# Soft-cap attention and a bilinear FFN on one core: first k load in two parts, cap loaded first, raw weights from the fifth on issued by SP

## The chip, the cores and the metric

The kernel runs on 1 core of one Trainium2 chip. The metric is device time in microseconds (us) of one execution, the median of several runs. A profile is one execution recorded by the hardware profiler. Its span goes from the first to the last instruction of the program.

## What is computed

```python
scale = 1.0 / np.sqrt(q.shape[-1])
scores = scale * np.matmul(q, k.transpose(0, 1, 3, 2))
scores = cap * np.tanh(scores / cap)
attn = softmax(scores)                       # exp, sum, divide
x = (attn @ v) -> 1792 tokens x 768
out = (x @ w_a) * (x @ w_b) @ w_out
```

q, k and v are 4 batches x 12 heads x 448 x 64 in float32, cap is one number, w_a and w_b are 768 x 1536 and w_out is 1536 x 768. The weights are float64: each raw weight block is loaded as pairs of 32-bit words and turned into float32 on the chip.

## The kernel before, in words

The 48 heads are worked in 24 pairs (`NPAIR`), two heads one above the other on the 128 partitions. The first 12 pairs (`NPG`) are group 0, the other 12 are group 1. For one pair `pi`:

- `load_k` (L204) loads k and q, each with four DMAs of 32 partitions, as blocks of 32 x 32 (packets of 128 bytes); `load_v` (L222) loads v. `turn` (L234) transposes the blocks on DVE, which gives k and q with the head's dimension on the partitions.
- `scores` (L258) multiplies them on PE in four chunks c, in the order 0, 1, 3, 2. `tanh` (L277) and `exp` (L285) run on ACT: tanh per chunk, exp per half (`hf`, two chunks). Two PSUM slots hold the scores, so chunk 3 waits for the tanh of chunk 0, and so on.
- `attend` (L301) multiplies with v on PE, in two halves. `add_full` and `add_last` (L289, L296) sum the probabilities on DVE, `sums` (L320) finishes the sum on PE.
- The sum's reciprocal goes through DRAM to reach all partitions: `recip` (L331, DVE), `store_rec` (L340, SP writes rd), `load_den` (L343, SP reads den back, two DMAs). Then `scale` (L356, DVE) gives x, and in group 0 `split_x` (L370, DVE) splits it into xhi and xlo, the operands of the FFN.

The FFN of a group needs the x of its pairs. `hidden` (L455) is one block of the first layer (18 matmuls in a row, tiles pha and phb), `project` (L486) one of the second layer. Its second token half (h = 1) needs xhi and xlo of pairs 6 to 11, pair 11 in the last three of its 18 matmuls. Weights come in the order `seq`, numbered t: `load64` (L385) loads the raw block (768 KB: 6 DMAs of 128 KB for t < 4, else 2 of 384 KB), `conv` (L402) makes float32 of it (two steps on ACT, three on DVE, one on POOL), `split_hi` and `split_lo` (L433, L443) make the PE operands. Two raw blocks fit at a time.

The order of work is planned before the program is written. Each step is a `job` with an engine, a cost, a lag and needs. The PE order is written out by hand (L663 to L701): it alternates `scores_of`, `attend_of`, `sums_of` and, from pair 12 on, pieces of the FFN (`ffn(us)` puts pieces worth that many us of PE). Every other engine takes, at each moment, the job with the earliest due time among those that can start. The loop at L824 writes all jobs in the order found, and each engine executes its own list in order. An engine's DMAs are issued in that list too. The semaphores of SP's and ACT's DMAs are eight in number and used in turn, so the ninth DMA of the two engines together is not issued before the first has landed.

`warm_up` (L741) issues memsets and matmuls on zeros before the first data. `limits` (L757) makes from cap the scale factors that tanh and exp read.

Of the kernel before, what the change touches and what calls it, by code (L numbers as in the profile page):

```python
# [119 lines left out]
def kernel(  # L120
# [403 lines left out]
    def loads(pi, heads):  # L524
        pairs = range(pi, pi + heads)
        for nm in "kq":
            eng = "ACT" if nm == "q" and pi < 2 else "SP"
            for n in range(P // BLK):
                free = [("turn", nm, p - NP) for p in pairs] if pi < NPG else [("turn", nm, pi - 1)]
                needs = [("load", nm, pi, n - 1)] if n else free  # L530
                job(("load", nm, pi, n), eng, 0.52, load_k, (pi, nm, n, heads), needs, 3.2 if pi < 2 else 4.0)
                jobs["load", nm, pi, n].order_only = n > 0
# [37 lines left out]
    def turns(pi):  # L570
        for nm in "kq":
            free = [("scores", pi - 2, c) for c in range(SUB)] + [("lo", nm, pi - 1)]
            job(("turn", nm, pi), "DVE", 0.56, turn, (pi, nm), [*(("load", nm, pi, n) for n in range(P // BLK)), *free])
# [85 lines left out]
    SOON, RAW, BACKLOG = 4.0, 24.0, 3.0  # L659
# [3 lines left out]
    for pi, heads in ((0, 1), (1, 1), *((i, 2) for i in range(2, NPG, 2)), *((i, 1) for i in range(NPG, NPAIR))):  # L663
# [22 lines left out]
    for pi in range(NPG, NPAIR + 1):  # L686
# [5 lines left out]
        if pi < NPAIR:  # L692
# [5 lines left out]
            ffn(GAP / 2 if pi > NPG else 7.2)  # L698
# [13 lines left out]
    for t, (nm, f, g) in enumerate(seq):  # L712
        if g == 0:
            parts = 6 if t < 4 else 2
            for n in range(parts):
                needs = [("raw", t, n - 1)] if n else [("conv", t - 2, 5)]
                job(("raw", t, n), "POOL" if t < 6 else "SP", 0.8 if t < 6 else 0.5, load64, (t, n, parts), needs, 4.0, RAW + 6.0 * (t + n / parts) if t < 4 else 0.0)
                jobs["raw", t, n].order_only = n > 0
            steps = (("ACT", 0.82), ("ACT", 0.8), ("DVE", 0.48), ("DVE", 0.48), ("DVE", 0.88), ("POOL", 2.1))
            for n, (eng, us) in enumerate(steps):  # L720
# [3 lines left out]
                job(("conv", t, n), eng, us, conv, (t, n), needs, 0.5)  # L724
# [15 lines left out]

    def warm_up():  # L741
        warm = bank(0, "warm")
        nc.vector.memset(psum[0][:, 0], 0.0)
        for n in (S, S, S, S // 2):
            nc.tensor.matmul(warm[:, :n], psum[0][:, 0, :P], psum[0][:, 0, :n], start=True, stop=True)
# [3 lines left out]
        nc.vector.memset(sel, 0.0)  # L749
        for z in kz:  # L750
            nc.vector.memset(f32(z), 0.0)
        nc.vector.memset(sel[:, Q - QS : Q], 1.0)
        nc.vector.memset(both, 0.0)
        for j, o in enumerate(own):
            nc.vector.memset(both[o, Q + (j - 1) * QS : Q + j * QS], 1.0)

    def limits():  # L757
# [5 lines left out]
        nc.vector.tensor_scalar_mul(capt[:, 1:2], capt[:, 6:7], 1.0 / math.sqrt(D))  # L763
        nc.scalar.activation(capt[:, 7:8], capt[:, 0:1], AF.Exp, scale=-1.0)
# [129 lines left out]
```

## Time and profile before

| | us |
|---|---|
| median of 3 runs | 717.94 |
| lowest, highest | 716.88, 720.42 |
| the profiled execution | 718.51 |
| its span | 716.7 |
| PE busy in the span | 703.4 (98%) |

A row of a timeline gives start, duration, engine, line, operation, output<-input, shape, count, and in brackets the idle time of the engine just before it with what ended it. The q behind an engine's name (SPq, ACTq) marks DMAs that it issues: the duration is that of issuing, not of the transfer. PEld is the loading of weights into PE, which overlaps the matmuls.

### The profile page before, as it was taken

The numbers are of one execution on the slowest core, as the hardware profiler recorded it, in microseconds if no ns is written. First come the engines' busy times: TensorE is split into PE (matmuls) and PEld (weight loads), VectorE is DVE, ScalarE is ACT, GpSimd is POOL, SyncE is SP. The second block draws the span as 40 slices with busy tenths as digits, with TensorE's granted clock in tenths as the row PEclk, the third lists the DMA queues.
The fourth block names the chain that finished last, engine by engine and source line by source line (L and its number), as shares of the span: only waits on it lengthen the run. The fifth ranks groups of instructions, "written<-read, shape, count | busy, mean of one in ns | idle before, by whom it ended". The sixth has DMA issues, their size and how long they took to land.

```text
span 716.7 us, 11238 instructions
## 1 busy us (share of the span) xinstructions
PE 703.4 (98%) x4370; PEld 578.3 (81%) x4370; DVE 423.0 (59%) x649; ACT 347.7 (49%) x474; POOL 112.0 (16%) x104
## 2 busy tenths in 40 slices
PE   7999998999999999999999999999999999999996
PEld 2333356879879789779879779999999999999996
DVE  4678897676679688686974849432043424434232
ACT  5989986577777566575646630222321112202100
POOL 0536431231322222222221100000000000000000
PEclk9999999999999999999999999999999999999999
DMA  9999585758777857858646437331022013101013
GB/s 128 152 171 170 140 212 123 193 143 200 184 170 193 193 141 177 201 138 227 157 116 159 146 101 248 110 109 45 11 83 83 23 34 99 53 15 44 1 45 113
DMA packets 142739, 90.55 MB, mean 126 GB/s; under 512 B 108024, under 2 KB 128536, under 8 KB 142680
## 3 DMA queue, kind: packets, MB, share of 16 engines
q1 hardware_dynamic: 135784, 82.53, 46.8%
q0 software_dynamic: 3040, 6.79, 4.0%
q10 hardware_dynamic: 3856, 0.46, 0.5%
q8 instruction: 36, 0.59, 0.4%
q14 instruction: 23, 0.19, 0.1%
HBM read 67.24 MB, written 22.50 MB: 125 GB/s over the span
## 4 chain that ended last, share of the span: by engine, by line
PE 92%; DMA 3%; SPq 2%; DVE 1%; ACT 1%; issue 0%; ACTq 0%; DVEq 0%
PE pv L308 10%; PE po L493 8%; PE po L494 8%; PE po L495 8%; PE phb L460 8%; PE phb L462 8%; PE phb L461 8%; PE pha L460 8%; PE pha L462 8%; PE pha L461 8%; PE psc L266 5%; PE psc L271 3%; DMA den<-rd 2%; PE pv L329 2%; SPq L220 1%; PE psc L274 1%
## 5 line engine op out<-in xcount | busy, mean ns | idle before, releaser
L493 PE MATMUL po<-who,gh 128*128 128x384 f32 x336 | 113.4, 337 | 0.0
L495 PE MATMUL po<-who,gl 128*128 128x384 f32 x336 | 112.5, 335 | 0.0
L494 PE MATMUL po<-wlo,gh 128*128 128x384 f32 x336 | 112.5, 335 | 0.0
L460 PE MATMUL pha<-xhi,wha 128*128 128x448 f32 x288 | 105.0, 365 | 2.7 <-DVE xhi L374 2.7
L460 PE MATMUL phb<-xhi,whb 128*128 128x448 f32 x288 | 105.2, 365 | 0.0
L462 PE MATMUL pha<-xhi,wla 128*128 128x448 f32 x288 | 104.8, 364 | 0.0
L461 PE MATMUL pha<-xlo,wha 128*128 128x448 f32 x288 | 104.6, 363 | 0.2 <-DVE xlo L375 0.2
L462 PE MATMUL phb<-xhi,wlb 128*128 128x448 f32 x288 | 104.6, 363 | 0.0
L461 PE MATMUL phb<-xlo,whb 128*128 128x448 f32 x288 | 104.3, 362 | 0.0
L283 ACT ACTIVATE pf<-psc,capt 128x896 f32<-128x896 f32 (+1 forms) x96 | 84.3, 909 | 29.6 <-PE psc L271 19.3
L308 PE MATMUL pv<-pf,vb 128*64 128x448 f32 x384 | 78.8, 553 | 0.0
L287 ACT ACTIVATE pf<-pf,capt 128x1792 f32<-128x1792 f32 (+1 forms) x48 | 77.1, 1606 | 0.8
L504 DVE TENSOR_TENSOR acc<-po,acc 128x384 f32<-128x384 f32 x84 | 46.4, 553 | 43.0 <-PE po L495 42.9
L467 ACT COPY asb<-pha 128x448 f32<-128x448 f32 x48 | 25.4, 531 | 81.8 <-PE pha L462 81.0
L493 PEld LDWEIGHTS po<-who,gh 128*128 128x128 f32 x336 | 63.1, 188 | 2.4 <-issue 1.2
L494 PEld LDWEIGHTS po<-wlo,gh 128*128 128x128 f32 x336 | 63.1, 188 | 0.1
L495 PEld LDWEIGHTS po<-who,gl 128*128 128x128 f32 x336 | 63.1, 188 | 0.0
L308 PEld LDWEIGHTS pv<-pf,vb 128*64 128x64 f32 x384 | 25.8, 139 | 45.5 <-issue 38.0
L477 DVE TENSOR_TENSOR asb<-phb,asb 128x448 f32<-128x448 f32 x48 | 29.9, 622 | 53.4 <-PE phb L462 53.4
L460 PEld LDWEIGHTS pha<-xhi,wha 128*128 128x128 f32 x288 | 54.0, 187 | 8.8 <-DVE xhi L374 3.4
L460 PEld LDWEIGHTS phb<-xhi,whb 128*128 128x128 f32 x288 | 54.0, 187 | 6.4 <-issue 2.5
L479 ACT CAST gh<-asb 128x448 fp32r<-128x448 f32 x48 | 27.2, 566 | 66.0 <-DVE asb L477 65.6
(103 smaller groups left out, 1038.4 us busy)
## 6 DMA issues: line engine op xcount, KB each, us to landing
w64o<-in_moe_w_out_dram SPq DMA_DIRECT2D x24, 384.0 KB
w64a<-in_moe_w_a_dram SPq DMA_DIRECT2D x18, 384.0 KB
w64b<-in_moe_w_b_dram SPq DMA_DIRECT2D x18, 384.0 KB
den<-rd SPq DMA_DIRECT2D x48, 112.0 KB
out_dram<-acc SPq DMA_DIRECT2D x13, 384.0 KB
wda<-wta SPq DMA_DIRECT2D x12, 384.0 KB
wdb<-wtb SPq DMA_DIRECT2D x12, 384.0 KB
wdo<-wto SPq DMA_DIRECT2D x12, 384.0 KB
```

Source lines behind the costliest of these rows:

```text
L266: nc.tensor.matmul(to, tk[o, at : at + (P if full else R)], tq[o], start=True, stop=True)
L283: nc.scalar.activation(to, prob.pop((pi, "s", c))[:, :n, :S], AF.Tanh, scale=capt[:, 1:2])
L287: nc.scalar.activation(pf, pf, AF.Exp, scale=capt[:, 0:1])
L308: nc.tensor.matmul(t[o, :S], tv[:, j * (NC3 + 1) + (c if j == 0 else (c + 1) % (NC3 + 1))], p, start=(c == 0), stop=(c == NC3))
L460: nc.tensor.matmul(t[:, :S], wh[:, kk], xhi[:, kk, cs], start=(kk == 0), stop=False)
L461: nc.tensor.matmul(t[:, :S], wh[:, kk], xlo[:, kk, cs], start=False, stop=False)
L462: nc.tensor.matmul(t[:, :S], wl[:, kk], xhi[:, kk, cs], start=False, stop=(kk == NK - 1))
L477: nc.vector.tensor_mul(t, phs.pop(("b", h))[:, :S], t)
L493: nc.tensor.matmul(t[:, :HALF], gh[:, cs], wh, start=(f == fs[0]), stop=False)
L494: nc.tensor.matmul(t[:, :HALF], gh[:, cs], wl, start=False, stop=False)
L495: nc.tensor.matmul(t[:, :HALF], gl[:, cs], wh, start=False, stop=(f == fs[-1]))
L504: nc.vector.tensor_add(acc[:, ti, hs], t, acc[:, ti, hs])
```

## The change

The planner gets other needs and costs, and with them the lists of all engines change.

- Pair 0's k is loaded in two parts: 192 of its 448 columns (`HEAD`) first, four DMAs on SP; the other 256 columns as `load2`, two DMAs on SP and two on POOL. `turn_head` transposes the first part, `turn` the rest. Chunk 0 of pair 0's scores needs only the first part.
- cap is loaded by POOL ahead of everything else; `limits` no longer needs the q of pair 0, and its last three instructions become a job of their own, `floors`.
- ACT issues only the q loads of pair 0. Those of pair 1 go to POOL. Pairs 2 and 3 are loaded one pair at a time and not together.
- The warm-up has ten matmuls of 128 columns in place of three of 448 and one of 224. Eight memsets go from DVE to POOL.
- On PE the first half of pair 0's `attend` comes before the scores of pair 1. In the first round of the FFN (pair 12), 3.6 us of FFN in place of 7.2 stand ahead of `attend` of pair 12.
- The raw blocks t = 4 and 5 are issued by SP and not by POOL. The planner's model holds back a DMA of SP or ACT while eight are on the way (`DEPTH`), and a conversion step on POOL counts a lag of 1.5 in place of 0.5.

```diff
+    HEAD = P + R
-    def load_k(pi, nm, n, heads):
+    def load_k(pi, nm, n, heads, part=None):
...
-        eng = nc.scalar if nm == "q" and pi < 2 else nc.sync
-        eng.dma_start(to.rearrange("p (c d) -> p c d", d=BLK), rows[:, h * BLK : (h + 1) * BLK].rearrange("(c p) d -> p c d", p=BLK))
+        eng = nc.gpsimd if part and n > 1 or (nm, pi) == ("q", 1) else nc.scalar if nm == "q" and pi < 1 else nc.sync
+        cs = slice(*((0, heads * S) if part is None else part and (HEAD, S) or (0, HEAD)))
+        to, rows = to[:, cs], rows[cs, h * BLK : (h + 1) * BLK]
+        eng.dma_start(to.rearrange("p (c d) -> p c d", d=BLK), rows.rearrange("(c p) d -> p c d", p=BLK))
+    def turn_head(pi, nm):
+        tt = qk.tile([P, S], F32, tag=f"t{nm}", name=f"t{nm}_{pi}")
+        nc.vector.transpose(tt[:, :HEAD], raw[nm, pi][:, :HEAD])
+        stk[nm, pi] = tt
     def turn(pi, nm):
         t = raw.pop((nm, pi))
+        if (nm, pi) in stk:
+            nc.vector.transpose(stk[nm, pi][:, HEAD:], t[:, HEAD:])
+            return
...
-        eng = nc.gpsimd if t < 6 else nc.sync
+        eng = nc.gpsimd if t < 4 else nc.sync
...
+                if (nm, pi) == ("k", 0):
+                    job(("load2", n), "POOL" if n > 1 else "SP", 0.52, load_k, (pi, nm, n, heads, 1), [("load", nm, pi, n)] if n < 2 else [], 3.2, 2.0 if n > 1 else 0.0)
...
-    def attend_of(pi):
-        for hf in range(2):
-            on_pe(("attend", pi, hf), 1.52, attend, (pi, hf), [("exp", pi, hf), *evac.get(pv_bank(pi), ()), *(("load", "v", pi, n) for n in range(4))])
+    def attend_of(pi, halves=(0, 1)):
+        for hf in halves:
+            on_pe(("attend", pi, hf), 1.52, attend, (pi, hf), [("exp", pi, hf), *(() if hf else evac.get(pv_bank(pi), ())), *(("load", "v", pi, n) for n in range(4))])
...
+    SOON, RAW, BACKLOG, DEPTH = 4.0, 24.0, 3.0, 8
-    for pi, heads in ((0, 1), (1, 1), *((i, 2) for i in range(2, NPG, 2)), *((i, 1) for i in range(NPG, NPAIR))):
+    for pi, heads in (*((i, 1) for i in range(4)), *((i, 2) for i in range(4, NPG, 2)), *((i, 1) for i in range(NPG, NPAIR))):
...
+        if pi == 1:
+            attend_of(0, (0,))
...
-            ffn(GAP / 2 if pi > NPG else 7.2)
+            ffn(GAP / 2 if pi > NPG else 3.6)
...
-                job(("conv", t, n), eng, us, conv, (t, n), needs, 0.5)
+                job(("conv", t, n), eng, us, conv, (t, n), needs, 1.5 if eng == "POOL" else 0.5)
...
+    def load_cap():
+        nc.gpsimd.dma_start(capt[:, 3:4], cap.rearrange("(a b) -> a b", b=1).to_broadcast([P, 1]))
     def warm_up():
+        load_cap()
         warm = bank(0, "warm")
-        nc.vector.memset(psum[0][:, 0], 0.0)
-        for n in (S, S, S, S // 2):
-            nc.tensor.matmul(warm[:, :n], psum[0][:, 0, :P], psum[0][:, 0, :n], start=True, stop=True)
+        nc.vector.memset(psum[0][:, 0, :P], 0.0)
+        for n in range(10):
+            nc.tensor.matmul(warm[:, :P], psum[0][:, 0, :P], psum[0][:, 0, :P], start=True, stop=True)
...
-    job("limits", "DVE", 1.3, limits, (), [("turn", "q", 0), "cap"])
-    jobs["tanh", 0, 0].needs.append("limits")
+    job("limits", "DVE", 1.0, limits, (), (), None, 4.0)
+    job("floors", "DVE", 0.4, floors, (), ["limits"])
+    for c in range(2):
+        jobs["tanh", 0, c].needs.append("floors" if c else "limits")
...
+        if x.move and x.eng != "POOL" and len(landed) >= DEPTH:
+            t = max(t, landed[-DEPTH])
```

**PE, first pairs.** In the lists below a tile's name is followed by its pair (psc_1_0 is chunk 0 of pair 1's scores, pf_0_1 the second half of pair 0's probabilities). Before:

```order
L266 MATMUL psc_0_2_251<-tq_0_216,tk_0_219 128x448 x2
L266 MATMUL psc_1_0_263<-tq_1_248,tk_1_255 128x448 x2
L266 MATMUL psc_1_1_267<-tq_1_248,tk_1_255 128x448 x2
L308 MATMUL pv_0_272<-pf_0_0_240,vb0_175 64x448 x4
L308 MATMUL pv_0_272<-pf_0_1_259,vb0_175 64x448 x4
```

And with the change:

```order
L277 MATMUL psc_0_2_263<-tq_0_238,tk_0_236 128x448 x2
L319 MATMUL pv_0_274<-pf_0_0_251,vb0_175 64x448 x4
L277 MATMUL psc_1_0_285<-tq_1_256,tk_1_269 128x448 x2
L277 MATMUL psc_1_1_290<-tq_1_256,tk_1_269 128x448 x2
L319 MATMUL pv_0_274<-pf_0_1_272,vb0_175 64x448 x4
```

The first half of pair 0's attend has moved ahead of pair 1's two score chunks.

**PE, around pair 12.** The first matmul of each block of 18 stands for the block (pha_0_0_1 is group 0, f = 0, token half 1). Before:

```order
L460 MATMUL pha_0_1_0_1290<-xhi_170,wha_0_1_1148 128x448
L460 MATMUL pha_0_0_1_1340<-xhi_170,wha_0_0_789 128x448
L308 MATMUL pv_12_1363<-pf_12_0_1231,vb0_175 64x448 x4
L308 MATMUL pv_12_1363<-pf_12_1_1287,vb0_175 64x448 x4
L329 MATMUL pv_12_1363<-psum0_165,sel_167 32x64 x14
L271 MATMUL psc_13_0_1411<-hq_13_1326,hk_13_1319 128x448 x2
```

And with the change:

```order
L471 MATMUL pha_0_1_0_1310<-xhi_170,wha_0_1_1164 128x448
L319 MATMUL pv_12_1354<-pf_12_0_1272,vb0_175 64x448 x4
L319 MATMUL pv_12_1354<-pf_12_1_1306,vb0_175 64x448 x4
L340 MATMUL pv_12_1354<-psum0_165,sel_167 32x64 x14
L282 MATMUL psc_13_0_1390<-hq_13_1346,hk_13_1336 128x448 x2
L471 MATMUL pha_0_0_1_1411<-xhi_170,wha_0_0_856 128x448
```

The block pha_0_0_1 has moved behind attend and sums of pair 12 and the first scores of pair 13.

**SP and ACT, around pair 12.** w64a_2 is the raw block t = 4, w64b_2 the block t = 5; rd11 and den_11 are the reciprocal's way through DRAM for pair 11. SP with the change (before, no w64 stands in this stretch: POOL issues both blocks):

```order
L408 DMA w64a_2_1167<-in_moe_w_a_dram 64x6x256 x2
L362 DMA den_9_1179<-rd9_102 64x448 x2
L362 DMA den_10_1193<-rd10_103 64x448 x2
L352 DMA rd11_104<-rec_11_1238 7x2x64
L362 DMA den_11_1289<-rd11_104 64x448 x2
L233 DMA vb2_177<-in_v_dram 128x3x64 x2
L235 DMA vb2_177<-in_v_dram 64x64 x2
L408 DMA w64b_2_1338<-in_moe_w_b_dram 64x6x256 x2
```

ACT, before:

```order
L409 ACTIVATE wtb_1_1159<-w64b_1_1023 128x768
L283 ACTIVATE pf_12_0_1231<-psc_12_0_1210,capt_132 128x896
L283 ACTIVATE pf_12_0_1231<-psc_12_1_1222,capt_132 128x896
L406 ACTIVATE w64a_2_1144<-w64a_2_1144 128x768
L287 ACTIVATE pf_12_0_1231<-pf_12_0_1231,capt_132 128x1792
L409 ACTIVATE wta_2_1274<-w64a_2_1144 128x768
```

And with the change:

```order
L420 ACTIVATE wtb_1_1198<-w64b_1_1050 128x768
L417 ACTIVATE w64a_2_1167<-w64a_2_1167 128x768
L294 ACTIVATE pf_12_0_1272<-psc_12_0_1229,capt_132 128x896
L294 ACTIVATE pf_12_0_1272<-psc_12_1_1241,capt_132 128x896
L420 ACTIVATE wta_2_1281<-w64a_2_1167 128x768
L298 ACTIVATE pf_12_0_1272<-pf_12_0_1272,capt_132 128x1792
```

On SP the fifth raw block stands ahead of den 9 and den 10, the sixth behind den 11. On ACT the first conversion step of the fifth block has moved ahead of the tanh of pair 12. On DVE, in both lists, scale of pair 11 comes first, then the last add of pair 12 (which sums of pair 12 needs), and the split of q of pair 13 behind them.

## Rows read from the trace of the kernel before

**Rows 1.** Page, part 1: busy time, share of the span, instructions.

```profile
PE 703.4 (98%) x4370; PEld 578.3 (81%) x4370; DVE 423.0 (59%) x649; ACT 347.7 (49%) x474; POOL 112.0 (16%) x104
```

**Rows 2.** Waits of PE, whole span: who <- whom: us in total, times, longest.

```profile
PE pha L460 <- DVE xhi L374: 2.7, 1, 2.7
PE psc L266 <- ACT pf L283: 2.1, 3, 1.3
```

**Rows 3.** Busy time by stretch: us, PE, PEld, DVE, ACT, POOL, PEclk, DMA share, GB/s.

```profile
2.00:5.00 3.00, 3.00 (x5) 1.35 (x4) 0.79 (x10) 0.00 (x0) 0.00 (x0) 1.00 1.21 167
...
14.70:96.00 81.30, 80.91 (x714) 30.13 (x715) 63.89 (x99) 75.86 (x73) 41.27 (x62) 1.00 0.93 159
...
132.00:430.00 298.00, 298.00 (x1869) 250.42 (x1867) 216.06 (x304) 189.66 (x276) 60.05 (x31) 1.00 0.66 169
```

**Rows 4.** Timeline of the first 18 us: PEld, DVE, ACT, PE.

```profile
5.29 0.34 PEld L745 LDWEIGHTS warm<-psum 128*128 128x128 f32 x1 [0.41 <-issue]
5.90 0.19 PEld L745 LDWEIGHTS warm<-psum 128*128 128x128 f32 x1 [0.27 <-issue]
...
6.11 0.65 DVE L237 STREAM_TRANSPOSE tq<-acc 128x448 f32<-128x448 f32 x1 [3.11 <-DMA capt<-in_cap_dram]
6.67 0.60 DVE L237 STREAM_TRANSPOSE tk<-acc 128x448 f32<-128x448 f32 x1
7.14 1.28 ACT L764 ACT_TABLE_LOAD   x1 [7.14 <-DMA acc<-in_q_dram]
...
7.33 1.77 PE L266 MATMUL psc<-tq,tk 64*128 64x448 f32 x8 [0.89 <-DVE capt L758]
...
10.46 1.79 ACT L287 ACTIVATE pf<-pf,capt 128x1792 f32<-128x1792 f32 x1
...
12.82 1.92 PE L266 MATMUL psc<-tq,tk 64*128 64x448 f32 x8 [1.32 <-ACT pf L283]
...
14.67 3.23 PE L308 MATMUL pv<-pf,vb 128*64 128x448 f32 x16
```

**Rows 5.** DMA issues of the first 20 us: KB each, median us to landing.

```profile
vb<-in_v_dram POOLq DMA_DIRECT2D x2, 96.0 KB, 3.0
```

**Rows 6.** Timeline of PE around pairs 11 and 12.

```profile
100.79 3.23 PE L308 MATMUL pv<-pf,vb 128*64 128x448 f32 x16
...
120.96 0.47 PE L460 MATMUL pha<-xhi,wha 128*128 128x448 f32 x1 [2.68 <-DVE xhi L374]
...
122.52 4.55 PE L308 MATMUL pv<-pf,vb 128*64 128x448 f32 x16
```

**Rows 7.** Timeline of SP, POOL, DVE and ACT there.

```profile
101.14 3.88 SPq L351 DMA_DIRECT2D den<-rd  x4
...
111.36 1.31 POOL L397 DMA_DIRECT2D w64b<-in_moe_w_b_dram  x2 [0.30 <-POOL wtb L420]
...
112.37 1.12 SPq L351 DMA_DIRECT2D den<-rd  x2
...
118.97 0.62 DVE L358 TENSOR_TENSOR den<-pv,den 128x448 f32<-128x448 f32 x1 [3.06 <-DMA den<-rd]
119.52 1.08 DVE L294 TENSOR_TENSOR psum<-psum,pf 128x896 f32<-128x896 f32 x1
...
105.67 1.91 ACT L283 ACTIVATE pf<-psc,capt 128x896 f32<-128x896 f32 x2 [2.52 <-PE psc L271]
...
113.07 1.43 ACT L287 ACTIVATE pf<-pf,capt 128x1344 f32<-128x1344 f32 x1
```

**Rows 8.** Chain of waits: two den transfers (start us, us); then DMA issues, 88 to 130.

```profile
95.37 2.25 DMA den<-rd
...
112.90 5.98 DMA den<-rd
...
w64a<-in_moe_w_a_dram POOLq DMA_DIRECT2D x2, 384.0 KB, 5.1
```

**Rows 9.** Waits of SP's queue, 0 to 130 us.

```profile
SPq L220 <- DVE tk L237: 7.2, 1, 7.2
```

More of the change, by code (lines that the diff above doesn't have):

```diff
@@ L526, in loads @@
         for nm in "kq":
-            eng = "ACT" if nm == "q" and pi < 2 else "SP"
             for n in range(P // BLK):
+                eng = "SP" if nm == "k" or pi > 1 else "POOL" if pi else "ACT"
                 free = [("turn", nm, p - NP) for p in pairs] if pi < NPG else [("turn", nm, pi - 1)]
-                needs = [("load", nm, pi, n - 1)] if n else free
-                job(("load", nm, pi, n), eng, 0.52, load_k, (pi, nm, n, heads), needs, 3.2 if pi < 2 else 4.0)
-                jobs["load", nm, pi, n].order_only = n > 0
+                needs = [("load", nm, pi, n - 1)] if n else [("load2", 3)] if (nm, pi) == ("q", 1) else free
+                args = (pi, nm, n, heads) if (nm, pi) != ("k", 0) else (pi, nm, n, heads, 0)
+                job(("load", nm, pi, n), eng, 0.52, load_k, args, needs, 3.2 if pi < 2 else 4.0)
+                jobs["load", nm, pi, n].order_only = n > 0 or (nm, pi) == ("q", 1)
+                if (nm, pi) == ("k", 0):
+                    job(("load2", n), "POOL" if n > 1 else "SP", 0.52, load_k, (pi, nm, n, heads, 1), [("load", nm, pi, n)] if n < 2 else [], 3.2, 2.0 if n > 1 else 0.0)
+                    jobs["load2", n].order_only = True
                 for p in pairs:
@@ L572, in turns @@
             free = [("scores", pi - 2, c) for c in range(SUB)] + [("lo", nm, pi - 1)]
-            job(("turn", nm, pi), "DVE", 0.56, turn, (pi, nm), [*(("load", nm, pi, n) for n in range(P // BLK)), *free])
+            free += [("load", nm, pi, n) for n in range(P // BLK)]
+            if (nm, pi) == ("k", 0):
+                job(("turn_head", nm, pi), "DVE", 0.28, turn_head, (pi, nm), free)
+                free = [("turn_head", nm, pi), *(("load2", n) for n in range(P // BLK))]
+            job(("turn", nm, pi), "DVE", 0.56, turn, (pi, nm), free)
             if pi >= NPG:
@@ L590, in scores_of @@
     def scores_of(pi, c):
-        ready = [("lo", nm, pi) for nm in "kq"] + ([("z", pi)] if c == NC3 else []) if pi >= NPG else [("turn", nm, pi) for nm in "kq"]
+        ready = [("lo", nm, pi) for nm in "kq"] + ([("z", pi)] if c == NC3 else []) if pi >= NPG else [("turn_head" if (nm, pi, c) == ("k", 0, 0) else "turn", nm, pi) for nm in "kq"]
         on_pe(("scores", pi, c), 0.6 if pi >= NPG else 0.76, scores, (pi, c), [*ready, *slots[-2:-1]])
         slots.append(("tanh", pi, c))
-    def attend_of(pi):
-        for hf in range(2):
-            on_pe(("attend", pi, hf), 1.52, attend, (pi, hf), [("exp", pi, hf), *evac.get(pv_bank(pi), ()), *(("load", "v", pi, n) for n in range(4))])
-        if pi in ON_PE:
+    def attend_of(pi, halves=(0, 1)):
+        for hf in halves:
+            on_pe(("attend", pi, hf), 1.52, attend, (pi, hf), [("exp", pi, hf), *(() if hf else evac.get(pv_bank(pi), ())), *(("load", "v", pi, n) for n in range(4))])
+        if pi in ON_PE and 1 in halves:
             on_pe(("sums_last", pi), 0.35, sums_last, (pi,))
@@ L671 @@
         if pi:
-            attend_of(pi - 1)
+            attend_of(pi - 1, (0, 1) if pi > 1 else (1,))
         for c in (3, 2):
@@ L716 @@
                 needs = [("raw", t, n - 1)] if n else [("conv", t - 2, 5)]
-                job(("raw", t, n), "POOL" if t < 6 else "SP", 0.8 if t < 6 else 0.5, load64, (t, n, parts), needs, 4.0, RAW + 6.0 * (t + n / parts) if t < 4 else 0.0)
+                job(("raw", t, n), "POOL" if t < 4 else "SP", 0.8 if t < 4 else 0.5, load64, (t, n, parts), needs, 4.0, RAW + 6.0 * (t + n / parts) if t < 4 else 0.0)
                 jobs["raw", t, n].order_only = n > 0
@@ L748, in warm_up @@
                 nc.vector.memset(t[own[1 - j], NC3 + j], 0.0)
-        nc.vector.memset(sel, 0.0)
+        nc.gpsimd.memset(sel, 0.0)
         for z in kz:
-            nc.vector.memset(f32(z), 0.0)
-        nc.vector.memset(sel[:, Q - QS : Q], 1.0)
-        nc.vector.memset(both, 0.0)
+            nc.gpsimd.memset(f32(z), 0.0)
+        nc.gpsimd.memset(sel[:, Q - QS : Q], 1.0)
+        nc.gpsimd.memset(both, 0.0)
         for j, o in enumerate(own):
-            nc.vector.memset(both[o, Q + (j - 1) * QS : Q + j * QS], 1.0)
+            nc.gpsimd.memset(both[o, Q + (j - 1) * QS : Q + j * QS], 1.0)
     def limits():
@@ L763, in limits, with floors @@
         nc.vector.tensor_scalar_mul(capt[:, 1:2], capt[:, 6:7], 1.0 / math.sqrt(D))
+    def floors():
         nc.scalar.activation(capt[:, 7:8], capt[:, 0:1], AF.Exp, scale=-1.0)
@@ L810 @@
             wait[x.eng].append(x)
-    order, port, moved = [], 0.0, 0.0
+    order, landed, port, moved = [], [], 0.0, 0.0
     MOVE = {load_k: 0.46, load_v: 0.5, load64: 1.7, store_rec: 0.15, load_den: 0.4, store_w: 1.0, reload_w: 1.0, store_x: 0.57, reload_x: 0.65, store_out: 1.0}
@@ L818, in starts @@
             t = max(t, moved - BACKLOG)
+        if x.move and x.eng != "POOL" and len(landed) >= DEPTH:
+            t = max(t, landed[-DEPTH])
         return t
     for x in real:
-        x.move = MOVE.get(x.fn, 0.0) * (x.args[3] if x.fn is load_k else 0.2 if x.fn is load_v and x.args[1] > 1 else 2 / x.args[2] if x.fn is load64 else 1.0)
-        x.shared = x.eng == "DVE" and x.fn not in (turn, recip, scale, collect) and not (x.fn is gate and x.args[3] == 0)
+        x.move = MOVE.get(x.fn, 0.0) * (x.args[3] * (1.0 if len(x.args) < 5 else 0.57 if x.args[4] else 0.43) if x.fn is load_k else 0.2 if x.fn is load_v and x.args[1] > 1 else 2 / x.args[2] if x.fn is load64 else 1.0)
+        x.shared = x.eng == "DVE" and x.fn not in (turn, turn_head, limits, floors, recip, scale, collect) and not (x.fn is gate and x.args[3] == 0)
     while len(order) < len(real):
@@ L839 @@
             x.end = max(x.end, moved + 0.7)
+            if x.eng != "POOL":
+                landed.append(t + x.us + 1.7 if moved < t + 1.6 + x.move else moved + 0.4)
         free[e] = t + x.us
```

5 lines of the change are left out of this document (removed).

## The prediction, made before the changed kernel ran

> **What bounds the kernel now.** I read the busy times first, then the list of waits, then the timelines of the places that the list names. PE is busy for 703.4 of 716.7 us [rows 1], so at most 13.3 us can be won without taking work from PE, and the change takes none but warm-up matmuls. In the stretches with nothing special PE has no gap: 80.91 of 81.30 us in group 0, 298.00 of 298.00 us in the FFN [rows 3]. A faster ACT, DVE or DMA there buys nothing. What is left is at two places: the start, with the first real matmul at 7.33 and two waits of up to 1.3 us for ACT behind it [rows 2, 4], and one stop of 2.68 us at 118, for xhi of pair 11, the longest wait of the list [rows 2, 6]. Both are what the change touches. A measurement of this kernel can tell about 0.5% (3.6 us) from no change.
>
> **The start.** The first scores start at 7.33, behind the turn of q (6.11 to 6.76) and that of k (6.67 to 7.27) [rows 4]. Both wait for their loads: eight DMAs of 56 KB, 448 KB together. With the change four of 24 KB and four of 56 KB come first, 320 KB. The other 128 KB are issued right behind and share the DMA engines. At the 167 GB/s of that stretch [rows 3] 128 KB are 0.8 us: all of it is saved if the parts stay in order, nothing if they mix. I take 0.5, in the middle, since each engine issues its first parts first. The turn of k's head can go before q has landed, so of the 0.60 us of k's turn [rows 4] some 0.5 leaves the path. The first scores start at 6.3, a gain of 1.0 (0.3 to 1.7).
>
> Three things must keep up. cap now comes by POOL: issued at about 0.7, landed 3.0 later by the nearest POOL issue [rows 5], then some 1.5 of small DVE instructions, done at 5.2, ahead of q's turn at 5.6. k's second part on POOL stands behind memsets: issued at about 2.8, landed at about 5.9, turned by 6.4, and chunk 1 wants it 0.8 after 6.3; the margin is 0.7. And the clock: a weight load took 0.34 us at 5.29 and 0.19 at 5.90 [rows 4], so the granted clock rose from 1.2 to 2.4 GHz in between, under warm-up matmuls from 1.40 on. The new warm-up has shorter matmuls and ends at about the same 5.4; I price a late rise at nothing and keep it as a rival.
>
> Behind the first scores, ACT's table load ended at 8.42 [rows 4], after the first chunk was there. It stands behind q(1)'s DMAs on ACT's queue, which now go to POOL, so tanh starts some 0.3 earlier. The first half of exp, which ended at 10.46 + 1.79 = 12.25, 4.9 behind the first scores [rows 4], ends 4.6 behind them. Before, PE did two more score chunks after a wait of 1.32 and stood at 14.67, 7.3 behind its start, with no attend done [rows 4]. Now half an attend (1.6, half of the 3.23 of [rows 4]) starts at 4.6, and the two chunks (1.8) end at 8.0 with those 1.6 done: level with 6.4. Gain 0.9. Its bounds are nothing (if PE waits for exp what it waited for tanh) and 2.1, all that PE waits for tanh [rows 2].
>
> The rest at the start costs nothing here: the loads of pairs 2 and 3 one pair at a time put eight more DMAs on SP, some 0.5 us of issuing each, beside PE's unbroken 14.7 to 96 [rows 3]; the memsets on POOL run before POOL has other work. If that cover is thin, pair 2's turn comes late and PE's next wait is for its k.
>
> **The stop at 118.** PE would have gone on at 120.96 - 2.68 = 118.28. Three matmuls are left of the block, at 0.2 each (16 in 3.23 [rows 6]), so attend of pair 12 was due at 118.9 and began at 122.52: 3.6 lost. It then took 4.55 where the same work took 3.23: 1.3 more, at a clock that had fallen in the stop [rows 6]. Together 4.9. The cause is den of pair 11: issued at 112.37, its transfer took 5.98 where another took 2.25, and scale waited for it until 118.97 [rows 7, 8]. In the same time POOL had the raw block t = 5 under way, issued at 111.36 [rows 7], two DMAs of 384 KB [rows 8].
>
> With the change the block that needs xhi of pair 11 stands behind attend, sums and first scores of pair 12, so five to seven us later. But the wait has a next in line: sums of pair 12 needs the last add, which stands behind scale on DVE. If den lands when it did, the add is done at 119.52 + 1.08 = 120.6 [rows 7]. Sums is due 3.4 behind attend, which now starts at about 115.0 (the block of 18 at 0.2, and 0.3 for its end, taken off 118.9): 118.4. So 2.2 would remain, and the clock might fall again.
>
> Two things move on SP. The block t = 5 is now issued behind den of pair 11, so den should take the 2.25 of the quiet transfer and land at 115.2 instead of 118.9. Against that, t = 4 stands on SP ahead of den 9, which was issued at 101.14 [rows 7]: issued at about 101.4, with 5.1 to landing [rows 8] it is there at 106.5. Its first conversion step on ACT now stands ahead of tanh of pair 12 (at 105.67 [rows 7]), so ACT runs late by 106.5 + 0.8 - 105.7 = 1.6. The second exp of pair 12, done at 113.07 + 1.43 = 114.5 [rows 7], is done at 116.1, still ahead of the second half of attend (116.6); DVE's adds behind it end at about 119.2, against 118.4. So 0.8 remains of the 4.9, and the gain is 4.1. Bounds: 1.4 (2.2 and 1.3 of clock remain) and 4.9.
>
> The eight that may be under way on SP and ACT hold the loads of pair 14 until t = 4 has landed, at about 106.5; pair 14 is a cycle of some 20 us away, so nothing. The planner's wait and POOL's lag of 1.5 only shift steps in unbroken stretches.
>
> **The sum.** The profiled execution took 718.5 us, 0.6 above the median of 717.9. 718.5 - 1.9 - 4.1 = 712.5; against the median 711.9.
>
> **Rivals.**
> Den lands no earlier. The row for it: den took 5.98 while POOL, another engine, had the transfers under way [rows 7, 8], so it was the traffic that was slow and not SP's queue. If the loads of pairs 13 and 14, which also stand there, are that traffic, nothing changes for den, and 2.2 to 3.5 stay in front of sums: 718.5 - 1.9 - 1.4 to 2.7, less 0.6 for the median: 713.3 to 714.6. The Trainium skill (DMA: Bandwidth & Descriptors, Issuing engines are not separate DMA queues) says that DMAs of all engines run on the same 16 DMA engines and interleave, and that another issuer saves only issue time. By that rule the move from POOL to SP is worth nothing in itself, and what counts is only that t = 5 is issued later; the rows agree so far.
>
> The start gives nothing: parts mix, or the clock rises late and the first scores run at the lower level, for 0.9 to 1.8 more. Then 711.9 + 1.9 = 713.8, or 714.8.
>
> Slower: SP held by a raw block. SP has been held once for 7.2 by a tile not yet free [rows 9]. A raw block may not be issued before the conversion of the one two before it, and that step is POOL's. On SP such a hold stops every load, rd and den behind it. If t = 4 is held until 105, it lands at 110, tanh of pair 12 follows at 111 in place of 105.67: with 1.6 of slack in ACT's list PE stops for about 4, and den 9 to 11 come late too, for another 4 to 6 and a clock fall of 1.3: 711.9 + 4.1 + 5.3 + 1.3 = 722.6. It decides where the hold is over 3 us. Against it: the step is done at about the time when POOL issued before, and the plan knows of it.
>
> The change doesn't do what it says: lists of all engines are new, and a small wait at some other turn eats the gain: about 717.5.
>
> **How the numbers follow.** Forecast 0.50 (own range 709.5 to 713.3), den no earlier 0.20, start without gain 0.10, no net gain 0.10, SP held 0.10. 0.5% faster is below 714.3: all of the forecast, half or more of the next two, so 0.64. Slower is the last, 0.09. The same: 0.27. The range goes from 709.5 (1.7 + 2.1 at the start and 4.9 at the stop, all upper bounds at once, would give 709.2) to 718.0, which leaves out the SP case.
>
> **What would show it.** Right: first scores at about 6.3 and attend ahead of pair 1's scores with no wait over 0.5 in the list; no wait for xhi; den of pair 11 in about 2.3 us; pair 12's attend in 3.23; at most 1 us in front of sums of pair 12; PE still unbroken behind 132. Wrong: a wait of sums for the add of 2 or more, den still at 5 to 6 us, waits of SP's queue for a raw tile, weight loads of 0.34 beside the first scores, or new waits for k, q or converted weights.

## The result and the profile after

The changed kernel takes 727.68 us (median of 4 runs, 725.77 to 730.20) against 717.41 for the kernel before on the same chip (4 runs): a ratio of 1.0137, 95% interval 1.0094 to 1.0180 (the ratio compares all runs and is not the quotient of the two medians). It is slower by 1.4%, above the forecast range. The profiled execution, the slowest of the four, has a span of 728.4 us, 11.7 more than before. The first part of its page shows that PE was busy for 4.1 us more than before [rows 1] and stood for 20.9 us in place of 13.3, 7.6 more; the busy time grew mostly because the clock fell behind two of the stops below, where before it fell behind one:

```profile
PE 707.5 (97%) x4382; PEld 580.7 (80%) x4382; DVE 422.9 (58%) x643; ACT 347.0 (48%) x474; POOL 117.4 (16%) x114
```

The waits of PE over the whole span (who waits, for whom: us in total, times, longest) say where. They answer to [rows 2]:

```profile
PE po L504 <- ACT gh L490: 4.9, 1, 4.9
PE psc L277 <- ACT pf L298: 2.0, 1, 2.0
PE pv L340 <- DVE psum L305: 1.7, 1, 1.7
PE po L504 <- DVE asb L488: 1.3, 1, 1.3
...
PE psc L277 <- DVE tq L248: 1.0, 1, 1.0
PE po L504 <- ACT who L451: 0.9, 1, 0.9
PE pv L319 <- ACT pf L298: 0.8, 1, 0.8
PE po L505 <- DVE wlo L459: 0.5, 1, 0.5
PE po L504 <- ACT acc L513: 0.4, 1, 0.4
```

The wait for xhi is gone. In its place stand one at the scores of pair 4 (33.6), one at the sums of pair 12 (121), and five at `project` (po), which never waited before, at 167 to 173 (three), 258 and 343. The stretch 300 to 380, in which PE used to have no gap [rows 3], reads (us, PE, PEld, DVE, ACT, POOL, PEclk, DMA share, GB/s):

```profile
300.00:380.00 80.00, 75.12 (x438) 62.46 (x438) 61.72 (x88) 48.84 (x72) 17.01 (x8) 0.96 0.66 168
```

The matmuls of `project` come in the same order in both traces, so their times tell how far PE is behind. The 193rd ends at 273.3 (269.6 before) and the 289th at 362.2 (350.5): 3.7 and 11.7 behind. The stop at 343, with what follows it, is 8.0 of the 11.7.

**The start** was gained, by less than forecast. PE, DVE and ACT there, which answer to [rows 4]:

```profile
6.71 4.17 PE L277 MATMUL psc<-tq,tk 64*128 64x448 f32 x16 [0.99 <-DVE tq L248]
11.67 1.72 PE L319 MATMUL pv<-pf,vb 128*64 128x448 f32 x8 [0.80 <-ACT pf L298]
13.33 1.77 PE L277 MATMUL psc<-tq,tk 64*128 64x448 f32 x8
15.03 1.72 PE L319 MATMUL pv<-pf,vb 128*64 128x448 f32 x8
```

```profile
5.37 0.14 DVE L793 TENSOR_SCALAR capt<-capt 128x1 f32<-128x1 f32 x1
5.55 0.38 DVE L239 STREAM_TRANSPOSE tk<-acc 128x192 f32<-128x192 f32 x1
6.01 0.65 DVE L248 STREAM_TRANSPOSE tq<-acc 128x448 f32<-128x448 f32 x1
```

The first scores start at 6.71. The turn of k's head did not go ahead of the path: it stood behind the limits on DVE (to 5.51), and q's turn behind it. The limits were late because POOL issued cap's load at 1.29, where 0.7 was forecast. At 15.03, with half an attend (1.6) done, PE stands level with 13.4, where it stood at 14.67 before: 1.2 won.

**The stop at 33.6** took that back twice over. DVE, then ACT, then PE:

```profile
33.29 0.65 DVE L248 STREAM_TRANSPOSE tk<-acc 128x448 f32<-128x448 f32 x1 [3.63 <-DMA acc<-in_k_dram]
...
34.83 0.63 DVE L248 STREAM_TRANSPOSE tq<-acc 128x448 f32<-128x448 f32 x1
```

```profile
33.09 1.01 ACT L294 ACTIVATE pf<-psc,capt 128x896 f32<-128x896 f32 x1 [0.32 <-PE psc L277]
34.12 1.42 ACT L298 ACTIVATE pf<-pf,capt 128x1344 f32<-128x1344 f32 x1
```

```profile
35.61 2.23 PE L277 MATMUL psc<-tq,tk 64*128 64x448 f32 x8 [1.99 <-ACT pf L298]
37.77 4.41 PE L319 MATMUL pv<-pf,vb 128*64 128x448 f32 x16
```

The list of waits names ACT's exp, which ended at 35.54. But these scores need no exp: from ACT they need only that a tanh has freed their slot, and the last tanh ended at 33.09 + 1.01 = 34.10. What they waited for is the turn of q, which ended at 34.83 + 0.63 = 35.46, behind a k of pair 4 that landed at 33.3. In e3, e4 and e10 below, which load the first pairs alike, the list names q's turn at this place. The attend behind the stop takes 4.41 where it takes 3.23 at full clock [rows 6] (granted clock 0.73 in 35.60 to 42.00), so the stop costs 3 in this execution. In the profiles of e3, e4 and e10 it is 1.35, 1.34 and 1.29 long and the clock does not fall behind it, so elsewhere it costs less.

**The stop at 343** is the dearest. ACT, then PE:

```profile
335.48 0.89 ACT L417 ACTIVATE w64b<-w64b 128x768 int32<-128x768 uint32 x1 [4.41 <-DMA w64b<-in_moe_w_b_dram]
...
340.72 0.92 ACT L417 ACTIVATE w64a<-w64a 128x768 int32<-128x768 uint32 x1 [1.97 <-DMA w64a<-in_moe_w_a_dram]
341.53 1.52 ACT L294 ACTIVATE pf<-psc,capt 128x896 f32<-128x896 f32 x2
...
343.39 1.43 ACT L298 ACTIVATE pf<-pf,capt 128x1344 f32<-128x1344 f32 x1
...
347.70 0.56 ACT L490 CAST gh<-asb 128x448 fp32r<-128x448 f32 x1
```

```profile
348.31 0.69 PE L504 MATMUL po<-who,gh 128*128 128x384 f32 x1 [4.88 <-ACT gh L490]
```

Behind the stop the clock is at the lower of its two levels (1.2 and not 2.4 GHz) for some six us; columns as above:

```profile
348.30:355.00 6.70, 6.69 (x19) 2.46 (x19) 6.38 (x12) 2.18 (x3) 0.10 (x1) 0.56 0.45 85
```

A granted clock of 0.56 over 6.7 us costs 2.9 us of work, beside the 4.88 of standing.

Twice ACT reaches the first conversion step of a raw block and stands there until the block lands, 4.41 and 1.97. At the second, the scores whose tanh is next in its list were done at 335. Behind that step come tanh, exp and several casts, and only then the gate's cast gh, for which PE waits. ACT's waits for raw blocks over the span are 30.6, 22.0 and 13.8, 66.4 together, where the kernel before has 47.7; with the change, then before:

```profile
ACT w64o L417 <- DMA w64o<-in_moe_w_out_dram: 30.6, 8, 7.9
ACT w64a L417 <- DMA w64a<-in_moe_w_a_dram: 22.0, 7, 6.4
...
ACT w64b L417 <- DMA w64b<-in_moe_w_b_dram: 13.8, 5, 4.4
```

```profile
ACT w64o L406 <- DMA w64o<-in_moe_w_out_dram: 18.4, 8, 5.1
ACT w64b L406 <- DMA w64b<-in_moe_w_b_dram: 15.3, 7, 7.0
ACT w64a L406 <- DMA w64a<-in_moe_w_a_dram: 14.0, 5, 5.7
```

### The profile page after: what moved, and what is told of

It reads as the page before. It is cut to its first block, busy times and chain, and to the rows that moved or that the text cites. A ratio compares the mean times of both kernels' runs of the same rounds, so it can differ in the third digit from the quotient of the medians.

```text
span 728.4 us, 11294 instructions
## 1 busy us (share of the span) xinstructions
PE 707.5 (97%) x4382; PEld 580.7 (80%) x4382; DVE 422.9 (58%) x643; ACT 347.0 (48%) x474; POOL 117.4 (16%) x114
## 3 DMA queue, kind: packets, MB, share of 16 engines
q0 software_dynamic: 2816, 5.51, 3.3%
## 4 chain that ended last, share of the span: by engine, by line
PE 71%; DMA 10%; ACT 8%; DVE 4%; SPq 3%; issue 3%; POOL 0%; ACTq 0%; DVEq 0%; POOLq 0%
PE po L504 8%; PE po L506 8%; PE po L505 8%; PE pv L319 7%; PE pha L471 6%; PE pha L473 6%; PE pha L472 6%; PE phb L473 5%; PE phb L471 5%; PE phb L472 5%; PE psc L277 4%; DMA w64a<-in_moe_w_a_dram 3%; ACT pf L294 3%; DMA w64o<-in_moe_w_out_dram 3%; PE psc L282 2%
## 5 line engine op out<-in xcount | busy, mean ns | idle before, releaser
L319 PE MATMUL pv<-pf,vb 128*64 128x448 f32 x384 | 81.2, 566 | 0.8 <-ACT pf L298 0.8
L490 ACT CAST gh<-asb 128x448 fp32r<-128x448 f32 x48 | 27.2, 566 | 66.4 <-DVE asb L488 66.1
```

The lines of the kernel that those rows point to most:

```text
L319: nc.tensor.matmul(t[o, :S], tv[:, j * (NC3 + 1) + (c if j == 0 else (c + 1) % (NC3 + 1))], p, start=(c == 0), stop=(c == NC3))
```

## The experiments

Each kernel is timed beside the kernel before on the same chip, which gave medians of 719.2 (e1 to e4), 719.8 (e5 to e8) and 719.2 (e9 to e12) on three chips. The ratio is the comparable number. A time below is the median. The stops are those of the profiled execution, which is the slowest of its kernel in the changed kernel, e1 (721.8) and e9 (726.4), and the fastest or second fastest in e6 (717.3), e8 (716.2) and e12 (713.1). The last two columns are sums over lists of waits, in us.

| | kernel | us | ratio, 95% interval | PE's waits at project | ACT's waits for raw blocks |
|---|---|---|---|---|---|
| | before | 717.4 | 1 | 0 | 47.7 |
| | the change | 727.7 | 1.0137 (1.0094 to 1.0180) | 8.0 | 66.4 |
| e1 | start part alone | 719.1 | 0.9992 (0.9970 to 1.0014) | 0 | 39.1 |
| e2 | pairs 2, 3 together | 726.0 | 1.0101 (1.0079 to 1.0123) | 9.4 | 69.0 |
| e3 | lag 0.5 | 716.2 | 0.9962 (0.9945 to 0.9979) | 0.6 | 49.8 |
| e4 | ACT's first step later | 719.5 | 1.0008 (0.9993 to 1.0023) | 1.5 | 45.7 |
| e5 | e2 and e3 | 714.6 | 0.9943 (0.9920 to 0.9966) | 0.2 | 52.4 |
| e6 | before, lag 1.5 | 720.1 | 1.0016 (0.9994 to 1.0038) | 1.5 | 53.4 |
| e7 | e5, blocks 4, 5 by POOL | 713.1 | 0.9935 (0.9912 to 0.9958) | 0 | 49.8 |
| e8 | e5, FFN 7.2 | 716.7 | 0.9972 (0.9957 to 0.9988) | 0 | 50.7 |
| e9 | e7, lag 1.5 | 723.5 | 1.0054 (1.0032 to 1.0075) | 7.6 | 59.6 |
| e10 | the change, lag 1.0 | 728.3 | 1.0125 (1.0090 to 1.0160) | 8.1 | 62.5 |
| e11 | e7, ACT's first step later | 713.0 | 0.9916 (0.9897 to 0.9936) | 0 | 35.2 |
| e12 | e7, raw block lands 0.7 later in the plan | 714.8 | 0.9953 (0.9934 to 0.9972) | 0.2 | 41.9 |

One part needs no run: without the rule of eight transfers (`DEPTH` so large that it never holds) the planner of the changed kernel writes the same list for every engine, row for row. It changed nothing there.

**e1**, the start part alone. The lines undone are those of e2, e3, e7 and e8, below, and `DEPTH`.

> Only the start part of the change stays (first k in two parts, cap by POOL, q of pair 1 by POOL, memsets, warm-up, first half of attend ahead of pair 1). Pairs 2 and 3 are loaded together again, the raw blocks 4 and 5 go back to POOL, 7.2 us of FFN stand ahead of attend of pair 12 again, the lag of POOL's conversion step is 0.5 and the rule of eight is off. Theory (the start gains 1.1 us up to 30 us, and all losses come from the other parts): 716.3, and none of the stops at 33.6, 168, 258 and 343. Rival (the start itself makes loads of pairs 4 and later late): the stop at 33.6 stays, 719 or more.

Neither. No stop at 33.6 and none at project, as the theory says, so the losses come from the other parts; but the time is level with the kernel before and not 1.1 under it. In the profiled execution, the slowest of the ten, the gain of the start is there until 115 and is lost in one wait, longer than the 2.68 of [rows 6]:

```profile
PE pha L471 <- DVE xhi L385: 4.7, 1, 4.7
```

Den of pair 11 was issued at 112.70 and scale began at 120.84, 8.1 later (6.6 before), with block 5 from POOL beside it. The runs lie between 714.5 and 721.8; that this wait makes the spread is not shown, since no fast one was profiled.

**e2**, pairs 2 and 3 together.

```diff
-    for pi, heads in (*((i, 1) for i in range(4)), *((i, 2) for i in range(4, NPG, 2)), ...
+    for pi, heads in ((0, 1), (1, 1), *((i, 2) for i in range(2, NPG, 2)), ...
```

> The changed kernel, with pairs 2 and 3 loaded together again (eight DMAs of 112 KB in place of sixteen of 56 KB). Theory (SP issues one DMA each 0.52 us, and with 56 KB each it cannot keep the DMA engines busy, so the k of pair 4 lands at 33.3): the stop of 1.99 at 33.6 and the slow clock behind it go, 3.0 us less: 724.5, with the stops at 168, 258 and 343 much as they were. Rival (the loads are late because of POOL's transfers or of waits on SP): the stop stays and the time is 727 to 728.

The stop at 33.6 is gone and those at project stay, as the theory has it. The time fell by 0.4% of the ratio, 2.6 us (1.7 in the medians), where 3.0 was expected; the two intervals overlap, so it is the profile that shows it. The stretch 9 to 18 of the three kernels, before, changed and e2 (columns as above), then two issues of SP in the changed kernel:

```profile
9.00:18.00 9.00, 7.20 (x36) 2.33 (x36) 5.06 (x7) 8.90 (x9) 0.55 (x1) 1.00 1.13 132
```

```profile
9.00:18.00 9.00, 8.16 (x38) 2.48 (x38) 5.76 (x8) 8.90 (x8) 1.71 (x3) 1.00 0.66 109
```

```profile
9.00:18.00 9.00, 8.11 (x39) 2.46 (x36) 5.62 (x8) 8.90 (x9) 1.77 (x3) 1.00 1.30 145
```

```profile
9.58 0.48 SPq L223 DMA_DIRECT2D acc<-in_k_dram  x1
10.10 0.48 SPq L223 DMA_DIRECT2D acc<-in_q_dram  x1
```

The share of the DMA engines fell to 0.66, with 109 GB/s, although SP issued without a gap, one DMA each 0.52 us (9.58, 10.10): at 56 KB each that is 108 GB/s. With 112 KB each the share is 1.30 and they move 145. The Trainium skill (DMA: Bandwidth & Descriptors, Issuing engines are not separate DMA queues) calls the issue time usually small relative to the DMA itself; here it set the rate.

**e3**, the lag of POOL's conversion step.

```diff
-                job(("conv", t, n), eng, us, conv, (t, n), needs, 1.5 if eng == "POOL" else 0.5)
+                job(("conv", t, n), eng, us, conv, (t, n), needs, 0.5)
```

> The changed kernel, with the planner's lag of POOL's conversion step at 0.5 again. Theory (the FFN stops come from lists that put ACT at a raw block just when it should land, and the longer lag makes more of them, 21 of 30 against 17 in the plan): the stop at 33.6 stays, those at 258 and 343 shrink: 720 to 724. Rival (the lag is harmless, the stops come from the smaller piece of FFN ahead of pair 12): within 1.5 of 727.5.

More than the theory expected: 1.75% in ratio, some 12 us, and faster than before. Of the waits at project 0.6 is left. The stop at 33.6 stays at 1.35. With a figure undone that exists only in the planner, the loss is gone.

**e4**, ACT's list alone. Only jobs of ACT change places:

```diff
+    for t in range(6, len(seq) // NG):
+        x, y = jobs["conv", t, 0], jobs["conv", t, 1]
+        order.remove(x)
+        order.insert(order.index(y), x)
     ET = mybir.EngineType
```

> The changed kernel with one change to ACT's list alone: the first conversion step of each raw block from the seventh on is moved right ahead of the second, so ACT does tanh, exp and the casts in between before it waits for the raw block. Theory (ACT stands at a raw block that has not landed, with tanh, exp and the gate's cast queued behind it): the stops at 258 and 343 go, 7 to 9 us less, 718.5 to 720.5. Rival (the ring of raw load, conversion and POOL step is itself too slow, ACT's place in it decides nothing): weights come later still, stops at the second layer stay or grow, 727 or more.

The theory holds: the stop at 258 is gone, that at 343 is down to 0.78, and 1.3% is won. The place of the stop at 343 on ACT now reads:

```profile
330.83 1.55 ACT L294 ACTIVATE pf<-psc,capt 128x896 f32<-128x896 f32 x2
...
335.53 0.91 ACT L417 ACTIVATE w64a<-w64a 128x768 int32<-128x768 uint32 x1
...
337.84 0.56 ACT L490 CAST gh<-asb 128x448 fp32r<-128x448 f32 x1
```

Tanh, exp and the casts run while the block is on its way, and when ACT comes to it there is no wait. The rival (the ring is too slow whatever ACT does) falls: the same raw loads, in the same lists of SP and POOL, are early enough.

**e5**, the lines of e2 and e3 together.

> The changed kernel with two parts undone: pairs 2 and 3 loaded together, the lag of POOL's conversion step at 0.5. Theory (these two parts make all of the loss, one at 33.6 and one in the FFN from 168 on): the 716.2 with the lag alone, less the 2.1 that pairs 2 and 3 together won up to 130 us: 714.1, with no stop at 33.6 and none over 0.6 behind 130. Rival (the two do not add up, since each new list of the planner is another draw): 716 or more, with a stop at a new place.

As the theory says: 714.6 (0.9943; the interval overlaps that of e3, 0.9962), no stop at 33.6, none over 0.2 at project. One stop of 1.52 is left, at the sums of pair 12.

**e6**, the line of e3 the other way round in the kernel before (0.5 becomes 1.5 for POOL).

> The kernel before, with nothing changed but the planner's lag of POOL's conversion step, 1.5 in place of 0.5. Theory (the longer lag puts raw loads later in SP's list while the conversion keeps its place on ACT, so ACT waits at raw blocks and PE stops behind it): stops behind 160, 721 to 729. Rival (the lag does harm only together with the shorter piece of FFN ahead of pair 12): 717.5 to 720.5.

The rival was right: the lag alone costs the kernel before nothing that can be told, with one stop of 1.54 at project (in an execution near the fastest; the runs go from 717.1 to 723.6).

**e7**, from e5, blocks 4 and 5 by POOL.

```diff
-        eng = nc.gpsimd if t < 4 else nc.sync
+        eng = nc.gpsimd if t < 6 else nc.sync
...
-                job(("raw", t, n), "POOL" if t < 4 else "SP", 0.8 if t < 4 else 0.5, ...
+                job(("raw", t, n), "POOL" if t < 6 else "SP", 0.8 if t < 6 else 0.5, ...
```

> As e5, with the raw blocks 4 and 5 issued by POOL again. Theory (block 5 beside den of pair 11 makes den late; on SP it stands behind den): the stop ahead of sums of pair 12 grows by 1 to 2.5 over that of e5, 715 to 716.5. Rival (block 4 on SP lands 2 to 3 us later than from POOL, and ACT stands at it with tanh of pair 12 behind): less of a stop than in e5, 1 us faster than e5.

The rival: the stop at the sums of pair 12 shrinks to 0.44. The times (712.8 to 716.9 against 714.0 to 715.7 in e5) overlap, so it is the profiles that show it. ACT in e5, then in e7:

```profile
106.63 0.91 ACT L417 ACTIVATE w64a<-w64a 128x768 int32<-128x768 uint32 x1 [4.80 <-DMA w64a<-in_moe_w_a_dram]
107.44 1.88 ACT L294 ACTIVATE pf<-psc,capt 128x896 f32<-128x896 f32 x2
```

```profile
104.21 1.91 ACT L294 ACTIVATE pf<-psc,capt 128x896 f32<-128x896 f32 x2 [2.42 <-PE psc L282]
106.01 0.89 ACT L417 ACTIVATE w64a<-w64a 128x768 int32<-128x768 uint32 x1
```

With block 4 on SP, ACT stands 4.80 at it with the tanh of pair 12 behind. From POOL it comes earlier and stands behind that tanh in the list: tanh starts 3.2 earlier.

**e8**, from e5, the longer piece of FFN.

```diff
-            ffn(GAP / 2 if pi > NPG else 3.6)
+            ffn(GAP / 2 if pi > NPG else 7.2)
```

> As e5, with 7.2 us of FFN ahead of attend of pair 12 again. Theory (the block that needs xhi of pair 11 then stands in front of den's landing once more): a wait for xhi of 1 to 3 and a slow clock behind it, 2 to 4 us more than e5. Rival (den is early enough with block 5 behind it on SP): no wait for xhi, within 1 of e5.

2.1 more than e5: the theory's time, not all of its reason. PE waits 1.83 for xhi, but scale of pair 11 (at 116.69) did not wait for den, which had landed 5.3 or less after its issue. It stood behind the adds on DVE, and these behind an ACT that had stood 4.62 at block 4. The times do not overlap (716.2 to 719.0 against 714.0 to 715.7 in e5).

**e9**, e7 with the lag at 1.5, the line of e3 back.

> As e7 (pairs 2 and 3 together, raw blocks 4 and 5 on POOL), but with the lag of POOL's conversion step at 1.5, so that this lag is the only difference from e7. Theory (the longer lag makes ACT's list stand at raw blocks in the FFN: 20 of 30 are planned with no room, 17 in e7): stops at the second layer behind 160, 5 to 12 us more than e7, 718 to 725. Rival (the lag does harm only with the other parts, as on the kernel before, where it cost nothing clear): 712.5 to 715.

10.4 more than e7 in the medians, 1.2% or some 9 us in the ratio, as the theory says. PE's longest waits in e9, of which e7 has none:

```profile
PE po L504 <- ACT gh L490: 3.3, 1, 3.3
PE po L504 <- DVE asb L488: 2.6, 1, 2.6
PE po L504 <- ACT acc L513: 1.5, 1, 1.5
```

**e10**, the change with the lag at 1.0 (`1.0 if eng == "POOL"`).

> The changed kernel with the lag of POOL's conversion step at 1.0, between the 0.5 that gave 716.2 and the 1.5 that gave 727.7. Theory A (the lag's own size counts): 720 to 724. Theory B (what counts is which list the planner happens to find; the lag is a draw): outside of that, near 716 or above 726.

728.3, outside what theory A allows: 0.5 is good, 1.0 and 1.5 are alike bad. The loss does not grow with the figure. It need not be a draw as B has it, either: by the measure below, 1.0 makes the raw blocks wait as long as 1.5.

**e11**, the lines of e4 on top of e7.

> e7 with ACT's first conversion step of each raw block from the seventh on moved right ahead of the second, as in e4. Theory (ACT's standing at raw blocks is what costs, and e7 has little of it left): 0 to 1 us less than e7, 712 to 713. Rival (the later first step makes the weights late): slower than e7 by 1 or more, with waits of PE for converted weights.

713.0, the time of e7 (the intervals of the ratios overlap), with no stop over 0.9 left, both of about that size at the start. ACT's waits for raw blocks fell from 49.8 to 35.2, and since PE no longer waited for any of it, nothing that can be told was won.

**e12**, e7 with a later landing in the plan.

```diff
-            x.end = max(x.end, moved + 0.7)
+            x.end = max(x.end, moved + (1.4 if x.fn is load64 else 0.7))
```

> e7 with one figure of the planner changed: a raw block counts as landed 0.7 us later, since the traces show 6.1 us from issue to ACT's first step at the least where the plan has 5.4. Theory (the plan's early landing is why ACT stands at raw blocks): ACT's waits for raw blocks shrink by half or more and the time is that of e7 or up to 1 less, 712 to 713.3. Rival (another list is another draw): a new stop, 715 or more.

In between: no stop over 0.6 behind the start (in the fastest of the executions), ACT's waits fell from 49.8 to 41.9 and not by half, and the runs spread from 713.1 to 718.4. A later landing in the plan did not pay here. The 6.1 was too much: for t = 6 to 35 in e7 the least from the start of SP's issue to ACT's first step is 5.9.

**What the lag does on the chip.** Worked out from the timelines of SP and POOL for the 30 raw blocks t = 6 to 35, as SP's issue of block t less the end of POOL's step of block t - 2, in the mean:

| kernels | lag | mean wait, us |
|---|---|---|
| e3, e5, e7, e1, e8 | 0.5 | 0.92, 0.96, 0.91, 1.07, 1.06 |
| the change, e2, e4, e9 | 1.5 | 1.58, 1.73, 1.55, 1.54 |
| e10 | 1.0 | 1.52 |
| before, e6 | 0.5, 1.5 | 1.15, 1.68 |

With the longer lag SP has other DMAs ahead of the raw block when its tile comes free (0.9 a turn in e7, 1.6 in e9). Two tiles go round, 15 turns each, so by an estimate 0.6 a turn makes a block up to 9 us later in the end: the first step of block 29 starts at 324.93 in e7 and at 336.74 in e9. Not all of that is the ring's, for PE itself is 7.2 later by then (the 241st matmul of project ends at 273.7 and 280.9).

The longer wait alone does no harm: e4 and e6 have it too, without the loss. PE stands only if something urgent is queued behind ACT's step. In the kernel before, ACT stands 5.66 at block 29, longer than at the stop of the changed kernel (4.41 and 1.97), and in e6 its step comes no later than there. But in both the gate's cast follows it soon in ACT's list; before, then e6:

```profile
336.16 0.89 ACT L406 ACTIVATE w64a<-w64a 128x768 int32<-128x768 uint32 x1 [5.66 <-DMA w64a<-in_moe_w_a_dram]
...
337.73 0.56 ACT L479 CAST gh<-asb 128x448 fp32r<-128x448 f32 x1
```

```profile
333.53 0.92 ACT L406 ACTIVATE w64a<-w64a 128x768 int32<-128x768 uint32 x1 [3.18 <-DMA w64a<-in_moe_w_a_dram]
334.35 0.56 ACT L479 CAST gh<-asb 128x448 fp32r<-128x448 f32 x1
```

In the changed kernel the gate's cast stands seven us of work behind that step (340.72 to 347.70). Read from the lists, the shorter piece of FFN shifts the scores against the FFN blocks, and this would be why the kernel before bears the lag. No run tested it by itself: e9 and e6 differ in the start part as well, and the new start with the longer piece of FFN and the lag at 1.5 was not run.

## Why the prediction was wrong

The forecast was 711.9, faster; it came out 727.7, slower. Point by point:

- **Step that failed, and most of the loss:** "The planner's wait and POOL's lag of 1.5 only shift steps in unbroken stretches." For the wait it was right. The lag cost 9 to 10 us (e9 against e7) to some 12 (e3), by making SP issue the raw blocks later while ACT's list had their first step ahead of tanh, exp and the gate's cast; taking away either of the two is enough (e3, e4). An unbroken PE [rows 3] was taken as cover; but PE was unbroken because the lists fitted, ACT's waits of 47.7 included, and the lists were what changed. The busy share of PE did not tell how much room the work beside it had.
- **Second step that failed:** pairs 2 and 3 one at a time, "some 0.5 us of issuing each", priced at nothing. The sixteen DMAs made SP's issue the limit (e2) and cost the stop at 33.6: 3 in the profiled execution, 1.7 to 2.6 in the times (e2). The sentence behind it named the sign, "pair 2's turn comes late"; it was pair 4's. The cover should have been counted as bytes by issue: 56 KB in 0.52 us is less than the 167 GB/s of [rows 3].
- **The start:** 1.9 forecast, 1.2 came. The 1.0 for the first scores came as 0.6, because k's head shared DVE with limits that cap had made late. The 0.9 for the half attend that starts early came as 0.6: the mechanism is right, but it started 5.0 behind the first scores and not 4.6, after a wait of 0.80.
- **The stop at 118:** 4.1 forecast. The wait for xhi went, and what is late next is the sums of pair 12, both as said; 1.69 was left and not 0.8. Where the text has ACT "late by 1.6" at block 4, tanh of pair 12 started at 111.30 and not at 107.3: SP issued the block at 103.55, where 101.4 was forecast, and ACT stood 4.17 at it, to 110.49. That block 5 behind den helps den is borne out by e8 (5.3 or less, against 6.6 before and 8.1 in e1, which differs from e8 only in who issues blocks 4 and 5 and in the rule of eight). But the move of the two blocks to SP loses more by block 4 than it gains by block 5 (e7, by the stops; the times overlap). What won at 118 is the shorter piece of FFN (2.1, e8).
- **The rivals:** "SP held by a raw block" had the nearest time, 722.6, and the right engine to be stopped, ACT ahead of tanh. The mechanism was another: SP's waits for POOL at raw blocks are 20.1 over the span, 26.6 before (sums of the rows of its lists of waits); the blocks were late through their place in the lists. "Lists of all engines are new, and a small wait at some other turn" was the true case, priced at 6 us instead of 16. ("The start gives nothing" has a slip in its sum: 713.8 with 0.9 to 1.8 more is 714.7 to 715.6, and not 714.8.)

## What to carry to other kernels

Where a planner writes the lists, a changed figure of the plan can change every list behind it: price it by what each in-order engine will stand at and what is queued behind that, not by how busy the slowest engine is. Put a wait for a transfer as late in an engine's list as its use allows, as e4 does; where PE waits for none of it, that wins nothing (e11). Splitting a load can make the issuing engine the limit: here 56 KB in 0.52 us were less than the DMA engines could move. Of this change the shorter piece of FFN is worth keeping (e8); the start with the early cap won 1.2 us in the profiles, but no time shows it (e1). With pairs 2 and 3 together, the lag at 0.5 and the blocks 4 and 5 on POOL (e7) they give 0.9935 of the kernel before, and with the first step late (e11) 0.9916, which can't be told apart.

## What the runs showed of the hardware

DVE can be slowed by POOL. In the changed kernel the last add of pair 17 (two instructions, 1.38 elsewhere) took 2.90 while POOL's conversion step ran; DVE first, then POOL:

```profile
255.62 2.90 DVE L310 SCALAR_TENSOR_TENSOR psum<-pf,capt,psum 64x448 f32<-64x448 f32 x2
```

```profile
255.92 2.11 POOL L431 TENSOR_TENSOR wtb<-wtb,w64b 128x768 int32<-128x768 int32 x1 [5.82 <-DVE wtb L428]
```

It is no single case: of the 33 such adds in that trace (line L310, one instruction each), the 23 that no conversion step of POOL touches took 0.69 at most, and each of the 8 that took 1.4 or more (up to 2.2) ran beside one. DVE ended the add above only at 258.5, the gate's step stood behind it, and PE's wait of 1.3 at 258 followed: with lists as tight as these such a collision reaches PE.
